# Loading the first block of an output projection unevenly over the DMA engines: 240 of its rows by sixes on 40 partitions

## The chip, the cores and the metric

One core of a Trainium2 chip runs the kernel. The metric is device time in microseconds (us) of one execution. Each comparison alternates the kernel before with the changed one on the same chip. Kernels are compared only within the same rounds. Traces are different: there is one trace of the kernel before.

## The reference, cut to what matters

The program is one decode step: an attention block over a long cache, and a small gated layer, mixed by a gate.

```python
B, Sq, D = 4, 1, 1024
H, Sk, Dh = 32, 8192, 128             # k_cache, v_cache: [B, H, Sk, Dh], 268 MB each, bf16
# wq: [D, H*Dh], wo: [H*Dh, D] (8 MB), w_gate, w_up: [D, 3584], w_down: [3584, D]

q = heads(x @ wq)
p = softmax(q . k_cache * Dh**-0.5)
o = p . v_cache
a = o.reshape(B, Sq, H * Dh) @ wo
b = x + y                             # y: a small gated layer on the same x  (cut)
return g * a + (1 - g) * b            # g = sigmoid(sum(x * gate_w))
```

Nearly all bytes are the two caches: 576 MB are read once, and each is used once. The last things needed are the last rows of v and then all of `wo`, in eight blocks of 1 MB (512 rows).

## The kernel before: the parts that matter

All large loads go into five slots of a ring in SBUF, and are issued by the sync engine in the order of use. A `wo` block lies on all 128 partitions, four rows (8 KB) on each.

```python
    TB = [const.tile([P, CJ * P], BF, name=f"TB{i}") for i in range(3)]   # three 8 KB-wide scratch tiles
    ...                                                                   # of the transposes of K, taken by turns
    def o_rows(g0, g1):                    # puts attention outputs into the row order of wo's blocks
        n = g1 - g0
        lp = small([P, FR, n, Bn])
        for k in range(WB):
            for r in range(FR):
                nc.tensor.matmul(lp[32 * k:32 * k + 32, r], lhsT=identb[:, r:P:FR],
                                 rhs=OT[:, WB * g0 + k:WB * g1:WB, :], start=True, stop=True, skip_group_check=True)
        nc.vector.tensor_copy(out=LT[:, :, g0:g1, :], in_=lp[:])

    def wo_block(g, r0=0, r1=FR):
        ...
        nc.sync.dma_start(out=w[:, r0:r1].rearrange("p r n -> p (r n)"),
                          in_=wov[:, g, r0:r1].rearrange("p r n -> p (r n)"))
        def use():
            for r in range(r0, r1):
                for n in range(NH):
                    mm_acc(acc[:, n * NB:(n + 1) * NB], LT[:, r, g, :], w[:, r, n * NB:(n + 1) * NB])
        return use
    ...
    for kind, d in order:                  # all pairs of K and V
        ...
        if (kind, d) == ("v", ND - 1):
            for g in range(2):
                wo_block(g)()              # blocks 0 and 1: loaded and used ahead of the last V pair
        if kind == "v":
            v_pair(d)
        ...
        if (kind, d) == ("v", ND - 2):
            o_rows(0, GE)
    last = [wo_block(g) for g in range(2, NWB - 2)]
    cuts = [(NWB - 2, 0, 2), (NWB - 2, 2, 4), (NWB - 1, 0, 2), (NWB - 1, 2, 3), (NWB - 1, 3, 4)]
    last += [wo_block(*cut) for cut in cuts]      # the last two blocks in pieces: 512, 512, 512, 256, 256 KB
    ...
    o_rows(GE, NWB)
    for use in last:
        use()
    res = turned(Bn, D)
    nc.vector.tensor_copy(out=res[:, 0:NB], in_=acc[:, 0:NB])
    nc.sync.dma_start(out=out2[:, 0:NB], in_=res[:, 0:NB])
    nc.scalar.copy(out=res[:, NB:D], in_=acc[:, NB:D])
    nc.scalar.dma_start(out=out2[:, NB:D], in_=res[:, NB:D])
```

## Time and profile before

| | before |
|---|---|
| time, median of the first 3 runs | 1343.82 us (1343.58 to 1344.03) |
| span of the profiled run (time 1343.99) | 1342.18 us |
| DMA, mean rate over the span | 429 GB/s |
| PE busy, DVE busy | 77%, 46% of the span |
| last landing of `wo` | 1338.71 us |
| last matmul ends | 1339.37 us |

These are lines of the page of the kernel before. The rows with 40 figures cut the span into equal slices; PEclk is the clock granted to TensorE in tenths. A queue line gives packets, megabytes and the share of the 16 engines' time.

```profile
PEclk9787988888998888889988889888889899888899
DMA  9999999999999999999999999999999999999997
GB/s 414 436 432 431 439 434 427 445 430 422 445 424 430 442 432 426 438 434 428 438 436 426 432 430 434 436 433 438 428 423 436 430 431 442 436 419 444 419 425 325
...
q1 hardware_dynamic: 14276, 575.69, 99.5%
q8 instruction: 27, 0.44, 0.1%
q14 instruction: 5, 0.04, 0.0%
```

The DMA engines are busy in every slice but the last, and one queue (q1, the loads) takes 99.5% of their time. PE and DVE have room on average. So compute does not set the pace of the body, and the change works on the tail. The last two lines are the fetching of instructions, 27 packets of 16 KB and 5 of 8 KB.

This is the chain of waits of the kernel before from 1330 us on: start, duration, what.

```profile
1321.33 16.11 DMA ring<-in_A_wo_dram
1337.43 0.04 issue
1337.47 1.90 PE acc L273 x8
1339.37 0.02 issue
1339.40 0.57 ACT TB L581
```

The last 512 KB and two 256 KB pieces of `wo` decide the end. At 1337.43 the 512 KB piece is complete, eight matmuls follow back to back, then a copy and the store. The last piece lands at 1338.71, and the last two of the eight matmuls start 0.05 us later: that landing is just in time, so both landings bind.

This is the timeline of PE of the kernel before from 1306 us on: start, duration, instruction and count; in brackets the idle time ahead of it and what ended it.

```profile
1306.60 2.75 PE L273 MATMUL acc<-ring,LT 128*4 128x512 bf16 x12 [0.32 <-DVE LT L370]
1308.98 0.39 PE L513 MATMUL o_ps<-ring,PB 128*32 128x512 bf16 x1
...
1313.84 7.07 PE L513 MATMUL o_ps<-ring,PB 128*32 128x512 bf16 x32 [1.23 <-DMA ring<-in_A_v_cache_dram]
1321.31 1.89 PE L513 MATMUL o_ps<-ring,PB 128*32 128x512 bf16 x8 [0.40 <-DMA ring<-in_A_v_cache_dram]
1323.80 1.89 PE L513 MATMUL o_ps<-ring,PB 128*32 128x512 bf16 x8 [0.61 <-DMA ring<-in_A_v_cache_dram]
1326.28 1.89 PE L273 MATMUL acc<-ring,LT 128*4 128x512 bf16 x8 [0.59 <-DMA ring<-in_A_wo_dram]
...
1333.75 5.61 PE L273 MATMUL acc<-ring,LT 128*4 128x512 bf16 x24 [0.36 <-DMA ring<-in_A_wo_dram]
```

PE starts the last V pair at 1308.98 and from there waits for data before nearly every piece: 1.23, 0.40, 0.61, 0.59 and 0.36 us. That idle time is what added PE work may use up.

One thing the page doesn't show is in the trace's landing records. Each DMA engine adds 1 to the transfer's semaphore when its share has landed, and each step has a time. For the last `wo` piece of the kernel before the 16 steps are:

| engines | landed at, us |
|---|---|
| seven, "early" | 1332.27 to 1333.18 |
| one, "middle" | 1335.31 |
| eight, "late" | 1336.93 to 1338.71 |

The piece is usable at the last of these. The spread, 6.4 us, was 0.6 us near the start and grew by about 1.5 us for an engine at each of the 27 fetches of q8; they fell on eight engines, the late ones. The same records point to what made the middle engine: one engine's lag steps from about 0.4 to 1.3, 2.2 and 3.1 us behind the first, in the first transfers to land after three of q14's five fetches (at 108.39, 564.44 and 991.41 us).

### The profile page before, as it was taken

The numbers are of one execution on the slowest core, as the hardware profiler recorded it, in microseconds if no ns is written. First come the engines' busy times: TensorE is split into PE (matmuls) and PEld (weight loads), VectorE is DVE, ScalarE is ACT, GpSimd is POOL, SyncE is SP. The second block draws the span as 40 slices with busy tenths as digits, with TensorE's granted clock in tenths as the row PEclk, the third lists the DMA queues.
The fourth block names the chain that finished last, engine by engine and source line by source line (L and its number), as shares of the span: only waits on it lengthen the run. The fifth ranks groups of instructions, "written<-read, shape, count | busy, mean of one in ns | idle before, by whom it ended". The sixth has DMA issues, their size and how long they took to land.

```text
span 1342.2 us, 7696 instructions
## 1 busy us (share of the span) xinstructions
PE 1032.8 (77%) x4552; PEld 227.9 (17%) x2364; DVE 614.4 (46%) x369; ACT 50.6 (4%) x46; POOL 62.8 (5%) x161
## 2 busy tenths in 40 slices
PE   2565878787788687778977779597778679877898
PEld 0111111111111121111211112111111112111221
DVE  2555655545336554335455556046555254556000
ACT  0000100001000010001000010000100010000100
POOL 2000100001000010001000010000100010000100
PEclk9787988888998888889988889888889899888899
DMA  9999999999999999999999999999999999999997
GB/s 414 436 432 431 439 434 427 445 430 422 445 424 430 442 432 426 438 434 428 438 436 426 432 430 434 436 433 438 428 423 436 430 431 442 436 419 444 419 425 325
DMA packets 14316, 576.18 MB, mean 429 GB/s; under 512 B 1598, under 2 KB 1606, under 8 KB 2252
## 3 DMA queue, kind: packets, MB, share of 16 engines
q1 hardware_dynamic: 14276, 575.69, 99.5%
q8 instruction: 27, 0.44, 0.1%
q14 instruction: 5, 0.04, 0.0%
q10 hardware_dynamic: 8, 0.00, 0.0%
HBM read 575.68 MB, written 0.01 MB: 429 GB/s over the span
## 4 chain that ended last, share of the span: by engine, by line
DMA 66%; DVE 21%; PE 11%; another core or an unknown queue 1%; ACT 0%; issue 0%; SPq 0%; DVEq 0%
DMA ring<-in_A_k_cache_dram 58%; DVE TB L436 21%; PE o_ps L513 9%; DMA ring<-in_A_v_cache_dram 5%; DMA x<-in_gate_w_dram 2%; DMA ring<-in_A_wo_dram 1%; PE S_ps L442 1%; ACT PB L484 0%; PE S_ps L307 0%; PE acc L307 0%; PE acc L273 0%; PE small L533 0%; ACT OS L525 0%; PE small L472 0%
## 5 line engine op out<-in xcount | busy, mean ns | idle before, releaser
L436 DVE STREAM_TRANSPOSE TB<-ring 128x2048 uint32<-128x2048 uint32 x256 | 566.9, 2277 | 492.4 <-DMA ring<-in_A_k_cache_dram 491.5
L442 PE MATMUL S_ps<-TB,Z 128*128 128x512 bf16 x2048 | 518.8, 408 | 219.4 <-DVE TB L436 218.9
L513 PE MATMUL o_ps<-ring,PB 128*32 128x512 bf16 x2048 | 461.4, 388 | 52.6 <-DMA ring<-in_A_v_cache_dram 48.1
L442 PEld LDWEIGHTS <-Z 128*128 128x128 bf16 x1024 | 105.4, 103 | 628.0 <-issue 626.4
L513 PEld LDWEIGHTS <-PB 128*32 128x32 bf16 x1024 | 100.7, 98 | 405.1 <-issue 393.7
L421 POOL COPY Z<-qa 32x4 bf16<-32x4 bf16 x128 | 25.6, 200 | 761.6 <-PE S_ps L442 736.0
L486 POOL COPY PB<-PT 32x1024 bf16<-32x1024 bf16 x16 | 30.3, 1892 | 430.3 <-PE o_ps L513 426.2
L467 ACT ACTIVATE PTs<-S_ps,mx 128x1024 bf16<-128x1024 f32 x8 | 8.9, 1114 | 1020.9 <-DVE mx L463 1020.9
L526 DVE SCALAR_TENSOR_TENSOR OS<-o_ps,mE,OS 128x512 f32<-128x512 f32 x8 | 6.0, 751 | 72.2 <-ACT OS L525 72.2
L484 ACT COPY PB<-PT 32x1024 bf16<-32x1024 bf16 x16 | 30.5, 1908 | 1.5 <-DVE PT L469 1.3
L474 DVE RECIPROCAL rinv<-small 128x16 f32<-128x16 f32 x8 | 2.1, 258 | 42.0 <-PE small L472 42.0
L370 DVE CAST LT<-small 128x64 bf16<-128x64 f32 x2 | 0.4, 224 | 42.3 <-PE small L368 42.3
L236 PE MATMUL small<-identb,x 6*128 6x6 bf16 x8 | 0.6, 195 | 22.3 <-DMA x<-in_gate_w_dram 22.3
L457 DVE TENSOR_REDUCE mx<-S_ps 128x1 f32<-128x1024 f32 x8 | 9.8, 1225 | 15.9 <-PE S_ps L442 15.9
L273 PE MATMUL acc<-ring,LT 128*4 128x512 bf16 x64 | 14.8, 379 | 1.7 <-DMA ring<-in_A_wo_dram 1.0
L469 DVE STREAM_TRANSPOSE PT<-PTs 128x1024 bf16<-128x1024 bf16 x8 | 10.0, 1245 | 10.2 <-ACT PTs L467 10.2
L273 PE MATMUL acc<-ring,hT 128*4 128x512 bf16 x56 | 12.2, 379 | 0.0
L525 ACT ACTIVATE OS<-o_ps,mE 128x512 f32<-128x512 f32 x8 | 5.5, 687 | 162.8 <-PE o_ps L513 162.8
L307 PE MATMUL o_ps<-ring,xw 128*4 128x512 bf16 x56 | 5.7, 536 | 5.3 <-DMA ring<-in_B_w_gate_dram 5.3
L533 PEld LDWEIGHTS small<-selg,OS 128*128 128x128 f32 x64 | 9.0, 208 | 4.1 <-issue 3.9
L533 PE MATMUL small<-selg,OS 128*128 128x16 f32 x64 | 8.7, 269 | 0.0
L238 DVE COPY xw<-small 128x48 bf16<-128x48 bf16 x1 | 0.2, 181 | 15.9 <-PE small L236 15.9
(64 smaller groups left out, 67.2 us busy)
## 6 DMA issues: line engine op xcount, KB each, us to landing
ring<-in_A_k_cache_dram SPq DMA_DIRECT2D x14, 4096.0 KB, 34.1
ring<-in_A_v_cache_dram SPq DMA_DIRECT2D x14, 4096.0 KB, 31.4
ring<-in_B_w_gate_dram SPq DMA_DIRECT2D x1, 7168.0 KB, 37.1
ring<-in_B_w_up_dram SPq DMA_DIRECT2D x1, 7168.0 KB, 39.2
ring<-in_B_w_down_dram SPq DMA_DIRECT2D x2, 3584.0 KB, 27.4
ring<-in_A_wo_dram SPq DMA_DIRECT2D x6, 1024.0 KB, 24.7
ring<-in_A_v_cache_dram SPq DMA_DIRECT2D x2, 2048.0 KB, 28.7
ring<-in_A_v_cache_dram SPq DMA_DIRECT2D x4, 1024.0 KB, 24.7
```

The source lines that it names most:

```text
L273: nc.tensor.matmul(out_ap, lhsT=lhsT, rhs=rhs, start=start, stop=True, skip_group_check=True)
L421: nc.gpsimd.tensor_copy(out=Z[at, :, QP - 1 + QP * q], in_=qa[at, :, h0 + q, b])
L436: nc.vector.transpose(out=flat_t.bitcast(U32), in_=kn[:, c * CJ * Dh:(c + 1) * CJ * Dh].bitcast(U32))
L442: nc.tensor.matmul(sps[:, z, :], lhsT=Z[:, he, s:s + P], rhs=T[:, 16 * z:16 * z + 16, half, :, e], start=(t == 0 and n == 0 and he == 0), ...
L457: nc.vector.tensor_reduce(out=mx[:, 0:1], in_=sps[:].rearrange("p z n -> p (z n)"), axis=AX.X, op=ALU.max)
L467: nc.scalar.activation(out=PTs[:], in_=sps[:].rearrange("p z n -> p (z n)"), func=ACT.Exp, bias=negm[:, 0:1], scale=scale, accum_out=rs[:, ...
L469: nc.vector.transpose(out=PT[:].rearrange("p j i -> p (j i)"), in_=PTs[:])
L484: nc.scalar.copy(out=Bv[at, :, :, q, :], in_=Pv[at])
L486: nc.gpsimd.tensor_copy(out=Bv[at, :, :, q, :], in_=Pv[at])
L513: nc.tensor.matmul(o_ps[row:row + NM, e, :], lhsT=PB[:, RD * t + c, z, w].rearrange("p e s j -> p (e s j)"), rhs=vn[:, j0 * Dh:(j0 + 4) * ...
L526: nc.vector.scalar_tensor_tensor(out=o_sb[:], in0=o_ps[:, 1, :], scalar=mE[:, 1:2], in1=o_sb[:], op0=ALU.mult, op1=ALU.add)
L533: nc.tensor.matmul(oT[:, :], lhsT=o_sb[:, q * Dh:(q + 1) * Dh], rhs=selg[:, q].rearrange("p t s -> p (t s)"), start=(q == 0), stop=(q == 3))
```

## The change

The intent follows from that table. If the early engines carried more of the bytes and the late ones fewer, all could end together. The change cuts `wo`'s first block (512 rows) in three. 240 rows, six to a partition, go on 40 partitions by two transfers whose source is counted in fives, so that only five engines carry them. 16 rows go on 16 partitions, and 256 rows by two on all 128. The wide rows need room, so the three scratch tiles become one. The rows of the attention output must be put in the new order too, by small matmuls with 0/1 matrices (`six`).

```diff
-    TB = [const.tile([P, CJ * P], BF, name=f"TB{i}") for i in range(3)]
+    TB = const.tile([P, 3, CJ * P], BF, name="TB")
@@ opening: 0/1 matrices, made on POOL (cut to its core)
+    six = const.tile([P, 2, 2, SX, 5, 4], BF)
+    ...
+    LX = const.tile([P, SX, Bn], BF)
+    LC = const.tile([16, Bn], BF)
+    L2 = const.tile([P, 2, Bn], BF)
@@ o_rows
+        if g0 == 0:
+            lp = small([P, SX + 3, Bn])
+            for h in range(2):
+                for r in range(SX):
+                    for k in range(2):
+                        nc.tensor.matmul(lp[32 * h:32 * h + 20, r], lhsT=six[:, k, h, r].rearrange("p e o -> p (e o)"),
+                                         rhs=OT[:, k, :], start=(k == 0), stop=(k == 1), skip_group_check=True)
+            ...                            # one matmul for the 16 rows, four for the 256, four copies to LX, LC, L2
+    def wo_first():
+        wo_home[0] = ring[:, slots(1)].rearrange("p (g r n) -> p g r n", g=4, r=FR)
+        n6, half = 40 * SX, P * FR // 2
+        w6 = TB[:].rearrange("p i n -> p (i n)")[:, 0:SX * D]
+        src = A_wo[0:n6].rearrange("(e h o r) n -> h e o (r n)", e=5, h=2, r=SX)
+        for h in range(2):
+            nc.sync.dma_start(out=w6[32 * h:32 * h + 20], in_=src[h])
+        w = wo_home[0][:, 0].rearrange("p r n -> p (r n)")
+        w2, wc = w[:, 0:2 * D], w[0:half - n6, 2 * D:3 * D]
+        nc.sync.dma_start(out=w2, in_=A_wo[half:2 * half].rearrange("(p r) n -> p (r n)", r=2))
+        nc.sync.dma_start(out=wc, in_=A_wo[n6:half])
+        def use():
+            ...                            # 12 matmuls with LX, 4 with L2, 2 with LC, where there were 8
@@ the loop
-            for g in range(2):
-                wo_block(g)()
+            wo_first()()
+            wo_block(1)()
```

The small table `row` of the opening also moves into the shared scratch tile (cut).

More of the change, by code (lines that the diff above doesn't have):

```diff
@@ L169 @@
     turn = [0]
-    TB = [const.tile([P, CJ * P], BF, name=f"TB{i}") for i in range(3)]
+    TB = const.tile([P, 3, CJ * P], BF, name="TB")
     tb_turn = [0]
     def turned(rows, n, dtype=BF):
-        t = TB[tb_turn[0] % 3]
+        t = TB[:, tb_turn[0] % 3]
         tb_turn[0] += 1
@@ L217 @@
     acc = acc4[0:Bn].rearrange("p z n -> p (z n)")
-    row = const.tile([P, 2, 32], F32)
+    row = turned(P, 64, F32).rearrange("p (i n) -> p i n", i=2)
     nc.vector.memset(row[:, 0, 0:1], 0.0)
@@ L233 @@
     nc.vector.tensor_copy(out=identb[:], in_=ident[:])
+    wide = turned(P, 3 * P)
+    nc.gpsimd.memset(wide, 0.0)
+    nc.gpsimd.tensor_copy(out=wide[:, P:2 * P], in_=ident[:])
+    SX = 6
+    six = const.tile([P, 2, 2, SX, 5, 4], BF)
+    for k in range(2):
+        for h in range(2):
+            at = P * (1 - k)
+            nc.gpsimd.tensor_copy(out=six[:, k, h], in_=wide[:, at:at + 240].rearrange("p (e h o r) -> p h r e o", e=5, h=2, o=4)[:, h])
+    LX = const.tile([P, SX, Bn], BF)
+    nc.gpsimd.memset(LX[:], 0.0)
+    LC = const.tile([16, Bn], BF)
+    L2 = const.tile([P, 2, Bn], BF)
     xw_ps = small([P, DT, NX], BF)
@@ L370, in o_rows @@
         nc.vector.tensor_copy(out=LT[:, :, g0:g1, :], in_=lp[:])
-    wo_home = {}
+        if g0 == 0:
+            lp = small([P, SX + 3, Bn])
+            for h in range(2):
+                for r in range(SX):
+                    for k in range(2):
+                        nc.tensor.matmul(lp[32 * h:32 * h + 20, r], lhsT=six[:, k, h, r].rearrange("p e o -> p (e o)"),
+                                         rhs=OT[:, k, :], start=(k == 0), stop=(k == 1), skip_group_check=True)
+            nc.tensor.matmul(lp[0:16, SX], lhsT=identb[:, P - 16:P], rhs=OT[:, 1, :], start=True, stop=True, skip_group_check=True)
+            for k in range(2):
+                for r in range(2):
+                    nc.tensor.matmul(lp[64 * k:64 * k + 64, SX + 1 + r], lhsT=identb[:, r:P:2], rhs=OT[:, 2 + k, :],
+                                     start=True, stop=True, skip_group_check=True)
+            for h in range(2):
+                nc.vector.tensor_copy(out=LX[32 * h:32 * h + 20], in_=lp[32 * h:32 * h + 20, 0:SX])
+            nc.vector.tensor_copy(out=LC[:], in_=lp[0:16, SX])
+            nc.vector.tensor_copy(out=L2[:], in_=lp[:, SX + 1:SX + 3])
@@ new lines @@
+    wo_home = {}
+    def wo_first():
[3 more added lines that the diff above has]
+        src = A_wo[0:n6].rearrange("(e h o r) n -> h e o (r n)", e=5, h=2, r=SX)
+        for h in range(2):
+            nc.sync.dma_start(out=w6[32 * h:32 * h + 20], in_=src[h])
[4 more added lines that the diff above has]
+        def use():
+            for r in range(SX):
+                for n in range(NH):
+                    mm_acc(acc[:, n * NB:(n + 1) * NB], LX[0:52, r, :], w6[0:52, r * D + n * NB:r * D + (n + 1) * NB])
+            for r in range(2):
+                for n in range(NH):
+                    mm_acc(acc[:, n * NB:(n + 1) * NB], L2[:, r, :], w2[:, r * D + n * NB:r * D + (n + 1) * NB])
+            for n in range(NH):
+                mm_acc(acc[:, n * NB:(n + 1) * NB], LC[:], wc[:, n * NB:(n + 1) * NB])
+        return use
```

## The prediction

> **What bounds the kernel now.** DMA: the page's slices show the 16 DMA engines 90% or more busy in all but the last, queue q1 at 99.5%, 429 GB/s; PE is busy 77%, DVE 46%. Only the tail can give time back. There the chain of waits is DMA wo to 1337.43 us, eight acc matmuls to 1339.37, a cast of 0.57, the store.
>
> The engines do not finish together. The trace's landing records (16 semaphore steps a transfer) show the last wo piece landing on seven engines at 1332.27 to 1333.18, on one at 1335.31, on eight at 1336.93 to 1338.71. That spread of 6.4 us was 0.6 at 38 us and grew in steps of about 1.5, one at each of the 27 instruction fetches (queue q8, 16 KB each): a data packet starts about 1.05 us late and takes 0.5 longer. They rotate over eight engines, the late eight. (The Trainium skill, "Runtime: NRT & Kernel Launch", Instruction fetch mechanics: blocks of 256 instructions, 16 KiB; the 27 packets agree.)
>
> **What the change does.** It loads the early engines more and the late ones less. The Trainium skill, "DMA: Bandwidth & Descriptors", Why a DMA increments its semaphore by 16: a sync-queue transfer runs on the largest number up to 16 that divides the slowest dimension of both sides, on the lowest-numbered engines. 20 partitions and fives give engines 0 to 4. The opening loads of x (4 and 1 landings) mark low engines: following their packets, I place three of engines 0 to 3 among those without fetches; the fourth is ambiguous.
>
> Wo's first MB per engine, by packet times (8 KB 0.31 us, 16 KB 0.61, 4 KB 0.16, 2 KB 0.08):
> - before: eight of 8 KB, 2.5 us.
> - after: engines 0 to 4 take eight of 12 KB (estimate 0.46 each), eight of 4 KB, one of 2 KB: 5.0; the others 1.36.
>
> The late eight end 1.1 us earlier (1337.6), engines 0 to 4 2.5 later (1334.8 to 1335.7), still before them. DMA gain: 1.1 us, all on the critical path.
>
> **What it adds.** PE: 29 small matmuls with weight loads (16 now take 0.65 us: estimate 1.2), four DVE copies of 0.2 (0.3 exposed), 18 accumulating matmuls instead of 8 at 0.2155: 2.2. PE starts the last V pair about 3.7 us later than 1309. Its slack there: idle 1.23, 0.40, 0.61, 0.59, then about 0.6 for each MB of wo. By that the lag is nearly gone at the last piece: the last matmul ends at 1338.3 (DMA) to 1338.8 (PE), against 1339.37. The main loop is unchanged: transposes wait on PE as with three separate buffers. The opening PoolE work hides under the first load. Eight semaphores reused over three more transfers still leave a backlog.
>
> **Predicted: 1343.0 us, range 1342.3 to 1344.0.** Chances: faster by over 2% 0.003, within 2% 0.992, slower 0.005.
>
> **What would show it.** Last piece's landings: two engines at 1331.8, one near 1334, five at 1335, eight to 1337.6, in place of 7/1/8. The w6 transfers: five landings each, 12 KB packets near 0.46 us. Still 27 fetches, the last some 8 us earlier. PE: waits in the last V pair (1.23, 0.40, 0.61) gone, those on the last wo pieces small. Main loop unchanged.
>
> **What would make it wrong.** If engines 0 to 4 hold a late one, the end moves out 2.5 us (about 1346). If PE's lag does not drain (throttled clock; it was full from 1268 on), the gain is lost: about 1344. If PE's lag is smaller, 1342.7.

## The result, and the profile after

| | before | after |
|---|---|---|
| time, median of 6 runs | 1343.86 us | 1343.82 us |
| range | 1343.58 to 1344.03 | 1343.67 to 1345.18 |
| span of the profiled run | 1342.18 | 1341.69 |
| its time | 1343.99 | 1343.71 |

The ratio is 1.0002, with a 95% interval of 0.9989 to 1.0015: the same. The time lies inside the predicted range, which says little, since the range holds the old time too. The forecast was a gain of 0.8 us, and hardly any came.

The page of the changed kernel, the same lines:

```profile
PEclk9787989988998898899988889898889799889999
DMA  9999999999999999999999999999999999999998
GB/s 415 438 430 431 439 434 426 438 430 428 436 432 429 439 434 424 440 430 436 436 426 432 432 432 438 436 427 431 436 424 435 436 427 445 431 423 434 429 422 334
...
q1 hardware_dynamic: 14358, 575.69, 99.5%
q8 instruction: 27, 0.44, 0.1%
```

The body is unchanged, the bytes are the same, there are still 27 fetches on q8. The DMA issues from 1270 us on show the new transfers (count, KB each; before there were three of 512 KB, and none of the last two lines):

```profile
ring<-in_A_wo_dram SPq DMA_DIRECT2D x4, 512.0 KB, 23.6
...
TB<-in_A_wo_dram SPq DMA_DIRECT2D x2, 240.0 KB
ring<-in_A_wo_dram SPq DMA_DIRECT2D x1, 32.0 KB, 28.3
```

The chain of waits of the changed kernel from 1330 us on:

```profile
1320.64 16.08 DMA ring<-in_A_wo_dram
1336.71 0.04 issue
1336.76 1.90 PE acc L287 x8
1338.66 0.02 issue
1338.68 0.57 ACT TB L636
```

It is the same chain, 0.72 us earlier at the DMA (1337.43 to 1336.71) and 0.71 at the end of PE. So the DMA did gain something. The timeline of PE:

```profile
1306.63 0.23 PE L395 MATMUL small<-OT,identb 128*64 128x4 bf16 x4
1307.32 2.75 PE L287 MATMUL acc<-TB,LX 52*4 52x512 bf16 x12 [0.46 <-DVE LX L398]
...
1312.12 0.39 PE L568 MATMUL o_ps<-ring,PB 128*32 128x512 bf16 x1
...
1313.00 12.90 PE L568 MATMUL o_ps<-ring,PB 128*32 128x512 bf16 x59
...
1331.08 7.57 PE L287 MATMUL acc<-ring,LT 128*4 128x512 bf16 x32 [0.36 <-DVE LT L384]
```

PE starts the last V pair at 1312.12, 3.1 us later than before (predicted: about 3.7), and the waits for V data are gone: 59 matmuls run through where there were 1.23, 0.40 and 0.61 us of idle. In the last group, 32 matmuls spaced 0.2155 us with a last one of 0.38 would take 7.06 us if they waited for nothing, and they take 7.57. So PE has about 0.5 us of waiting left, and the DMA still sets the end.

The landing records of the last `wo` piece:

| engines | before, us | after, us |
|---|---|---|
| early | seven at 1332.27 to 1333.18 | three, not used by the new rows, at 1331.37 to 1331.70 |
| the "middle" one | 1335.31 | **1338.00**, the last of all |
| late, the three last of them | to 1338.71 | 1337.39, 1337.59, 1337.68 |
| the other nine (late ones and early ones now loaded) | | 1335.33 to 1336.32 |

The late engines end 1.03 us earlier, as predicted (1337.6 forecast, 1337.68 measured). But the middle engine moved out by 2.69 us and is now last. So the landing gain is 0.71 us in this trace in place of 1.1.

The profiled pair also shows where that 0.71 us went. The span gained only 0.48 us, and the time only 0.28 us:

| step | before | after | change |
|---|---|---|---|
| last matmul ends | 1339.37 | 1338.66 | -0.71 |
| store landed to the sync engine's closing drain | 0.08 | 0.32 | +0.24 |
| time minus span | 1.80 | 2.02 | +0.22 |

(Time minus span is the mean over the runs of both kernels; in the profiled pair alone it is 1.82 and 2.02.) At the end the sync engine waits for the eight DMA semaphores in turn, by number, 101 to 105 and 108 to 110. Before, the two output stores were on 109 and 110, the last of the list. The three extra transfers turned the assignment on by three, the stores are on 102 and 103, and the remaining waits come after the store has landed.

So the theory (A) is: the placement of the middle engine cost the DMA part of its gain, and 0.24 us inside the span and 0.22 us outside it (time minus span; whether before or behind it, no trace shows) ate the rest. The rival is (B): PE, which got about 3 us more work, is what keeps the end. (C) is no rival but the part of A about the end: that the closing waits come from the semaphores' order alone.

### The profile page after: what moved, and what is told of

The parts are those of the page before. It is cut to its first block, busy times and chain, and to the rows that moved or that the text cites. A ratio compares the mean times of both kernels' runs of the same rounds, so it can differ in the third digit from the quotient of the medians.

```text
span 1341.7 us, 7789 instructions
## 1 busy us (share of the span) xinstructions
PE 1038.0 (77%) x4591; PEld 228.6 (17%) x2398; DVE 615.2 (46%) x373; ACT 50.6 (4%) x46; POOL 64.6 (5%) x168
## 4 chain that ended last, share of the span: by engine, by line
DMA 68%; DVE 20%; PE 11%; ACT 0%; issue 0%; SPq 0%; DVEq 0%
DMA ring<-in_A_k_cache_dram 58%; DVE TB L491 20%; PE o_ps L568 8%; DMA ring<-in_A_v_cache_dram 6%; DMA ring<-in_B_w_gate_dram 3%; PE S_ps L497 2%; DMA ring<-in_A_wo_dram 1%; PE o_ps L321 0%; ACT PB L539 0%; PE acc L321 0%; PE acc L287 0%; PE small L588 0%; ACT OS L580 0%; PE small L527 0%; SPq L560 0%
## 5 line engine op out<-in xcount | busy, mean ns | idle before, releaser
L491 DVE STREAM_TRANSPOSE TB<-ring 128x2048 uint32<-128x2048 uint32 x256 | 566.8, 2277 | 490.8 <-DMA ring<-in_A_k_cache_dram 490.8
```

The source lines that it names most:

```text
L491: nc.vector.transpose(out=flat_t.bitcast(U32), in_=kn[:, c * CJ * Dh:(c + 1) * CJ * Dh].bitcast(U32))
```

## The experiments

Eighteen kernels ran, in five lots. Each lot shares its runs of the kernel before.

### First lot: repeat, engine ruler, PE alone, DMA alone

**a1_after_again**: the changed kernel once more.

> The changed kernel once more, for a second trace and an interval. Theory A (one of engines 0 to 4 is the middle engine of before, and with 2.7 us more it becomes the last one): the last wo piece lands last on that engine, near 1338.0, the late eight by 1337.7, and the time is 0.5 to 0.7 us under before. Theory B (the matmul work that was added takes the gain): the last landing is as early, but the last matmul ends more than 0.66 us after it. If the medians differ by under 0.2 us while the trace's end is 0.5 earlier, something outside the traced span or a spread between runs takes the rest.

Measured: median 1343.96 us against 1343.88 before (ratio 0.9999, 0.9986 to 1.0013; all five runs, 1343.68 to 1344.11). The middle engine is again last, at 1338.35, and the late ones end at 1337.97. In the chain the DMA ends at 1337.07. So the gain of the DMA in this run is only 0.36 us, and the end costs 0.25 and 0.21 again: the three sum to +0.1, as measured. The 0.5 to 0.7 us under before that I expected of the time did not come. The DMA gain of one and the same kernel thus varies by about 0.35 us from trace to trace.

**a2_ruler**: which engine is the middle one? The kernel before, with eight small loads of 1 to 8 partitions, ahead of `wo`. A load of k partitions is carried by the k lowest-numbered engines (the Trainium skill, "DMA: Bandwidth & Descriptors", Why a DMA increments its semaphore by 16; here the loads of 1 to 8 partitions indeed show that many landings; the numbers of the engines are the page's, the trace has only the landings).

```diff
+            for i, k in enumerate((1, 2, 3, 4, 5, 6, 7, 8)):
+                nc.sync.dma_start(out=TB[i // 4][0:k, (i % 4) * D:(i % 4 + 1) * D], in_=A_wo[0:k])
```

> The kernel before with eight tiny loads in front of wo, 1 to 8 partitions of 2 KB, so that each lands on 1 to 8 engines, counted from the lowest if the rule holds. Each landing time places one engine among the sixteen of the transfer before. Theory A: among engines 0 to 4 four stand with the early seven and one with the middle engine, about 3.0 us behind; no engine of 0 to 7 but that is late. Rival (all five early): engines 0 to 4 all within 0.9 us of the first. Time within 1 us of before.

Measured: one run, 1347.94 us, 4.1 us over before, where I had expected 1 at most. The loads of 1, 2 and 3 partitions have all landed by 1294.27; the load of 4 has three landings with those and a fourth at 1295.61. So engine 3 is the middle engine. The load of 5 adds an early landing at 1293.54: engine 4 is early. The loads of 6 and 7 add landings at 1299.18 and 1297.36: engines 5 and 6 are late. My expectation on the last point was a miss. In one respect this run cannot serve: the sync engine waited for the ruler loads, the engines fell into step, and the spread of the `wo` transfers that followed collapsed from 6.5 to 0.65 us (1.6 to 1.8 in the last six, after one more fetch). The time rose all the same.

**a3_pe_only**: all the added PE, DVE and POOL work, with the DMA of before. Five rows of zero weights (`L0`) stand in for the extra matmuls, so the result stays right.

```diff
-            for g in range(2):
-                wo_block(g)()
+            wo_first()()      # the old single transfer of block 0, its 8 matmuls, and 10 more with L0 = 0
+            wo_block(1)()
```

> Wo's first block loaded as before in one transfer, but with all matmuls, copies and setup of the change (10 of the 18 accumulating matmuls have zero weights, so the result is right). Theory A: the added matmul work drains in the tail, last matmul about 0.66 us after the last landing, time within 0.2 us of before. Theory B: 0.5 to 0.8 us slower than before.

Measured: median 1343.88, the same as before (ratio 1.0000, 0.9988 to 1.0013); the last landing is at 1338.63, the DMA in the chain ends at 1337.35, time minus span is 1.81. The PE work costs nothing at the DMA's old pace. This speaks against B.

**a4_dma_only**: the DMA of the changed kernel, with the matmuls of before. The result is wrong: block 0's matmuls read rows in the wrong places.

```diff
-        if g0 == 0:
-            ...                                 # all small matmuls and copies for LX, LC, L2
-            for r in range(SX):
-                ...                             # LX, L2 and LC matmuls
+            wr = wo_home[0][:, 0]
+            for r in range(FR):
+                for n in range(NH):
+                    mm_acc(acc[:, n * NB:(n + 1) * NB], LT[:, r, 0, :], wr[:, r, n * NB:(n + 1) * NB])
```

> The four transfers of the change, but no added matmuls: the block is used as before from the ring, which holds other data there, so the result is wrong on purpose. Theory A: no better than the changed kernel, 0.5 to 0.7 us under before in the trace, last landing at 1338.0 on the middle engine. Theory B: 0.5 us or more faster than the changed kernel of the same rounds.

Measured: median 1343.94 (ratio 1.0000, 0.9987 to 1.0012), no better than the changed kernel. The last landing is at 1338.27 on the middle engine, the chain's DMA ends at 1336.99, time minus span is 2.03. So without any of the added PE work the gain is missing just as well. B is refuted for this change: the loss lies in the DMA and in the end.

### Second lot: the end, the middle engine, PE's lag

**b1_after_plus5** and **b2_before_plus3**: tiny loads that nothing reads, long before the end, shift only which semaphores the stores get. Five in the changed kernel put them back on 109 and 110; three in the kernel before put them on 102 and 103.

```diff
+    idle = const.tile([1, 5, 16], BF)
+    def tiny():
+        for i in range(5):                      # range(3) in the kernel before
+            nc.sync.dma_start(out=idle[:, i], in_=A_wo[i:i + 1, 0:16])
@@ the loop
+        if (kind, d) == ("k", 12):
+            tiny()
```

> The changed kernel with five loads of 32 bytes in mid-run, so that it issues eight transfers more than before in place of three, and its two stores signal on the last two of the eight transfer semaphores again, as before. Theory C (the end costs more when the stores' semaphores stand earlier in the order in which the end waits for them): the sync engine's last waits after the stores land shrink by 0.25 us, time minus traced span returns from 2.02 to 1.80 us, and the time is 0.4 to 0.5 us under the changed kernel: 1343.4 to 1343.5. Rival (the gain is lost elsewhere): unchanged, 1343.8 to 1344.0.

> The kernel before with three loads of 32 bytes in mid-run: nothing else of the change. Theory C: the stores' semaphores move as in the change; last waits 0.25 us longer, time minus span 2.02 us, time 0.4 to 0.5 us over before: 1344.3 to 1344.4. Rival: same as before, 1343.9.

Measured: b1 has a median of 1343.51 against 1343.91 for the kernel before of these rounds (ratio 0.9997, 0.9984 to 1.0009). From the landed store to the drain it is 0.08 us again. b2 has a mean of 1344.22 against 1343.94, +0.28, with its waits at the end back (0.32 us), and time minus span at 1.78. So the in-span part of C is shown both ways: 0.25 us from nothing but a shifted order. The later runs happen to give the steps between: from the landed store to the drain it is 0.08 us with the stores' semaphores not shifted, 0.19 with a shift by one (c1, d2, d3), 0.25 by two (d1), 0.32 by three and 0.34 by four (d6). The other part fell: time minus span of b1 is 2.016, not back to 1.80. That 0.22 us is not the store's semaphore.

The chain of b1 from 1330 us on, to compare with the changed kernel (1336.71):

```profile
1320.68 16.07 DMA ring<-in_A_wo_dram
1336.75 0.04 issue
1336.79 1.90 PE acc L287 x8
```

**b3_threes**: does it help to spare engine 3? The same with fewer engines: 192 rows by eights on 24 partitions, source in threes (engines 0 to 2), 64 rows on 64 partitions, the five tiny loads, and the small matmuls one V pair earlier.

```diff
-    SX = 6
-    six = const.tile([P, 2, 2, SX, 5, 4], BF)
+    SX = 8
+    six = const.tile([P, 2, 2, SX, 3, 4], BF)
-        n6, half = 40 * SX, P * FR // 2
+        n6, half = 24 * SX, P * FR // 2
-            nc.sync.dma_start(out=w6[32 * h:32 * h + 20], in_=src[h])
+            nc.sync.dma_start(out=w6[32 * h:32 * h + 12], in_=src[h])
@@ and 64 rows for LC, with the five tiny loads
-        if (kind, d) == ("v", ND - 2):
+        if (kind, d) == ("v", ND - 3):
             o_rows(0, GE)
```

> Twelve partitions a transfer with a source in threes, so three engines (0 to 2) and not the middle engine 3: 192 rows by eights on 24 partitions, 64 rows on 64 partitions; its small matmuls moved one V pair earlier, where PE waits anyway; five tiny loads for the semaphores. Theory A: w6 lands three times, all within 0.9 us; the middle engine stays about 3.2 us behind the first; the last landing is on a late engine with four fetches, 0.9 us earlier than before, near 1337.8; engines 0 to 2 near 1337.2. With theory C time 1342.9 to 1343.2. If PE's lag now matters, the last matmul ends more than 0.7 us after the last landing.

Measured: 1344.23 median (ratio 1.0004), a miss. What A says of the engines held: three landings within 0.96 us, the middle engine untouched at +3.02. But the last landing is at 1338.56 on a late engine (1337.8 expected): the late ones did not come forward. The rate shows a loss. These are windows of one microsecond; the last two figures of each line are the DMA engines' busy share and GB/s. The kernel before:

```profile
1298.00:1299.00 1.00, 0.00 (x0) 0.00 (x0) 0.00 (x0) 0.00 (x0) 0.00 (x0) 1.00 0.99 418
1299.00:1300.00 1.00, 0.93 (x5) 0.19 (x2) 0.00 (x0) 0.00 (x0) 0.00 (x0) 1.00 0.94 393
1300.00:1301.00 1.00, 1.00 (x6) 0.19 (x2) 0.00 (x0) 0.00 (x0) 0.00 (x0) 1.00 1.09 459
```

And b3_threes:

```profile
1298.00:1299.00 1.00, 1.00 (x7) 0.19 (x2) 0.00 (x0) 0.00 (x0) 0.00 (x0) 1.00 1.22 348
1299.00:1300.00 1.00, 1.00 (x6) 0.19 (x2) 0.00 (x0) 0.00 (x0) 0.00 (x0) 1.00 0.84 262
1300.00:1301.00 1.00, 1.00 (x6) 0.29 (x3) 0.00 (x0) 0.00 (x0) 0.00 (x0) 1.00 0.97 320
```

The engines stay busy but move 930 KB in place of 1270 in these 3 us. The packets of 8 KB in these 3 us took a median of 0.406 us, 0.313 in the kernel before. At 429 GB/s the missing 340 KB are, as an estimate, 0.8 us of the whole core's DMA, about what the redistribution was to win. The changed kernel moved 1231 KB there. Of what differs from it, two things are suspected: the 64 rows on 64 partitions, and the step of 128 KB from one engine's source rows to the next one's (96 KB in the change). c2 and c3 below pick that up.

**b4_early**: b1, with the small matmuls one V pair earlier. If PE's lag were the loss, taking about a microsecond from it would show.

```diff
-        if (kind, d) == ("v", ND - 2):
+        if (kind, d) == ("v", ND - 3):
             o_rows(0, GE)
```

> As b1, with the small matmuls and copies of the change one V pair earlier, where PE waits for data. PE's lag at the last V pair shrinks by about 1.5 us. If that lag costs nothing (theory A) same as b1 within 0.15 us; if PE's lag costs (theory B) 0.2 us or more under b1.

Measured: median 1343.46 (ratio 0.9996, 0.9984 to 1.0009), within 0.1 us of b1. PE's lag is not the loss. In this trace the middle engine's offset was smaller, 2.68 us when the new transfers began, and the last landing, 1337.79, is the earliest of the five traces with exactly these transfers (1337.79 to 1338.35). In these five the last landing follows the middle engine's offset in the V transfer just ahead of the new ones:

| | b4 | b1 | change | a4 | a1 |
|---|---|---|---|---|---|
| middle engine behind the first, us | 2.68 | 3.05 | 3.11 | 3.29 | 3.43 |
| last landing of `wo`, us | 1337.79 | 1338.02 | 1338.00 | 1338.27 | 1338.35 |

That is what A asks for, and the 0.35 us between traces go with it. Why the offset varies is open.

b1 and b4 are the best versions found. Each of their ten runs (at most 1343.62) is below each of the nine runs of the kernel before of the same rounds (at least 1343.69). The means differ by 0.44 and 0.48 us, 0.03 to 0.04%, which is inside the formal interval of the ratio.

### Third lot: which engines, which shape

**c1_shape_probe**: one tiny load of 20 partitions with its source in fives, in the kernel before. Does that shape alone lengthen the time outside the span?

```diff
+    idle3 = const.tile([20, 8], BF)
+    def tiny():
+        src = A_wo[0:240].rearrange("(e h o r) n -> h e o (r n)", e=5, h=2, r=6)
+        nc.sync.dma_start(out=idle3[:], in_=src[0][:, :, 0:8])
```

> The kernel before with one tiny load in mid-run, of the shape of the change's w6 transfers (20 partitions, source in fives, 16 bytes a partition). It asks whether that shape alone makes the end after the traced span longer. If it does: time minus span 2.02 us. If not: 1.80 us, and the longer end belongs to something else in the changed transfers. The stores' semaphores move by one, so the span itself may grow by 0.1 to 0.25 us.

Measured: median 1343.96 us, the same as before; time minus span 1.80. The shape alone does not.

**c2_fours**: engines 0 to 3: 192 rows by sixes on 32 partitions, and 64 rows on 64 partitions as in b3. The tiny loads and the early small matmuls are kept in all of c2, c3 and c4.

```diff
-    six = const.tile([P, 2, 2, SX, 5, 4], BF)
+    six = const.tile([P, 2, 2, SX, 4, 4], BF)
-        n6, half = 40 * SX, P * FR // 2
+        n6, half = 32 * SX, P * FR // 2
-            nc.sync.dma_start(out=w6[32 * h:32 * h + 20], in_=src[h])
+            nc.sync.dma_start(out=w6[32 * h:32 * h + 16], in_=src[h])
```

> Sixteen partitions a transfer, source in fours: engines 0 to 3, 192 rows by sixes on 32 partitions, 64 rows on 64 partitions; small matmuls early, five tiny loads. Theory A: w6 lands four times, the fourth about 2.5 to 3 us behind, so the middle engine is one of 0 to 3, and it is last, near 1338.0. For the miss of the threes: if loading 64 rows to 64 partitions was what slowed all engines there (port theory), the slump of the bandwidth between 1298 and 1301 us comes again, and the late engines end 0.5 us or more after 1337.8; if it was the source's step of 128 KB (step theory; here 96), the bandwidth stays above 360 GB/s and they end by 1337.9.

Measured: median 1344.73 against 1343.96 (ratio 1.0005). The first two transfers have four landings, the fourth 3.55 and 3.81 us behind the first: the middle engine is one of 0 to 3, which agrees with the ruler. It is last again, at 1339.34. The rate sags again at the same place:

```profile
1298.00:1299.00 1.00, 0.71 (x4) 0.10 (x2) 0.00 (x0) 0.00 (x0) 0.00 (x0) 1.00 1.08 354
1299.00:1300.00 1.00, 0.41 (x2) 0.10 (x1) 0.00 (x0) 0.00 (x0) 0.00 (x0) 1.00 0.90 322
1300.00:1301.00 1.00, 1.00 (x6) 0.19 (x2) 0.00 (x0) 0.00 (x0) 0.00 (x0) 1.00 1.11 406
```

**c3_threes10**: engines 0 to 2 again, but the 240 rows of the change, by tens on 24 partitions, and only 16 rows on 16 partitions.

```diff
-    SX = 6
-    six = const.tile([P, 2, 2, SX, 5, 4], BF)
+    SX = 10
+    six = const.tile([P, 2, 2, SX, 3, 4], BF)
-        n6, half = 40 * SX, P * FR // 2
+        n6, half = 24 * SX, P * FR // 2
```

> Threes again, but 240 rows by tens on 24 partitions and the other 16 rows on 16 partitions as in the change. Theory A: the middle engine keeps 3.0 us; engines 0 to 2 take 5.0 us more and land between 1337.3 and 1338.2. Port theory: no slump below 360 GB/s from 1298 to 1301, the late engines end by 1337.7, time 1343.2 to 1343.6. Step theory: also none (step 160 KB). If the slump comes, few engines reading large rows are the cause.

Measured: median 1344.01 of six runs, 1343.77 to 1349.85, against 1343.96. Expected was 1343.2 to 1343.6: a miss. The deep sag is gone (342, 440 and 410 GB/s in the three windows, 1192 KB together, where b3 had 930 and c2 1082), and the middle engine stays at +3.30. The source's step is 128 KB in b3, 96 in c2 and 160 in c3, so it does not sort them. The sag goes with the 64 rows on 64 partitions, a transfer that is also four times as large as the 16 rows of c3. The Trainium skill, "SBUF — State Buffer", Door 1, says that the partitions a transfer spans decide how many of the 16 ports into the memory it reaches, and that partitions 0 to 63 reach half of them. The sag with b3 and c2 fits this. But the 16 partitions of c3 reach fewer ports still and carry a quarter of the bytes, so ports and size are not told apart; that the ports are the cause was not tested by itself.

The profiled run of c3 happens to be the one of 1349.85, so its trace tells little about the end, but it shows another danger. Windows of it (the figure before the DMA share is the granted clock):

```profile
1260.00:1300.00 40.00, 38.92 (x219) 10.94 (x145) 1.08 (x6) 0.98 (x1) 0.41 (x1) 0.85 1.00 424
1300.00:1313.00 13.00, 13.00 (x62) 2.75 (x30) 0.00 (x0) 0.00 (x0) 0.00 (x0) 1.00 1.00 423
1313.00:1320.00 7.00, 7.00 (x23) 1.05 (x11) 0.00 (x0) 0.00 (x0) 0.00 (x0) 0.52 1.01 418
```

The clock was halved for 7 us in the very stretch in which PE must catch up, and it was low from 1260 to 1300 too (0.85; 0.96 in b4). The last landing was at 1338.15, but PE ended at 1345.03, 6.9 us behind it. This is one run. That the other single slow runs (1345.18 of the changed kernel, 1345.03 of b3, 1345.33 of c3) have the same reason is not known, since they were not profiled. Their mean clocks of 0.897 to 0.901 are ordinary, but 7 us at half the clock change such a mean by less than 0.003.

**c4_mixed**: a split load: 120 rows by sixes in fives, 120 rows by tens in threes, so that engine 3 gets half as many extra bytes.

```diff
-    six = const.tile([P, 2, 2, SX, 5, 4], BF)
+    SH = ((5, 6), (3, 10))
+    six = const.tile([P, 2, 2, 120], BF)
...
+        for h, (e, r) in enumerate(SH):
+            src = A_wo[120 * h:120 * h + 120].rearrange("(o e r) n -> e o (r n)", o=4, e=e)
+            nc.sync.dma_start(out=w6[32 * h:32 * h + 4 * e, 0:r * D], in_=src)
```

> The first 120 rows by sixes in fives (engines 0 to 4), the next 120 by tens in threes (engines 0 to 2), so the middle engine 3 gets only one of the two; other rows as in the change; small matmuls early, five tiny loads. Theory A: middle engine ends near 1336.2, engines 0 to 2 by 1337.2, last landing on a late engine near 1337.65, 1.05 us before that of before; with the end 0.22 us longer the time is 1343.0 to 1343.2, under b4. Rival: 1343.4 or more.

Measured: median 1343.87 (1343.44 to 1344.36) against 1343.96, expected 1343.0 to 1343.2: a miss. On the DMA it did what it should: the last landing is at 1337.79 on a late engine, 0.92 us earlier than before, and the middle engine is no longer last. But the chain now holds no DMA at its end:

```profile
1331.55 7.08 PE acc L290 x32
1338.63 0.02 issue
```

32 matmuls run back to back for 7.08 us, which is the time that 32 need without any wait. The 26 matmuls that the mixed first block takes (18 in the change) have pushed PE behind: PE starts the last V pair at 1312.60, in b4, with 18, at 1311.01. It ends 0.84 us after the last landing. So here rival B is true. Its size in this trace is 0.18 us: b4 has its last landing at 1337.79 as well and ends at 1338.45. But the profiled run is the fastest of the five, so what keeps the median 0.4 us above it is not shown. The room for added PE work ends between the change and c4. c3 has the same 26 matmuls, so its miss may have this cause too; none of its ordinary runs was profiled.

### Fourth and fifth lot: what lengthens the time outside the span

Time minus span is 2.01 to 2.05 us in the changed kernel, a1, a4, b1, b3, b4, c2, c3 and c4, and 1.78 to 1.81 in the kernel before, a2, a3, b2 and c1. So it goes with the changed transfers. The last six runs added these to the kernel before one kind at a time (two rows-by-six transfers, halves, 16 rows), then together; extra rows are read by nothing.

```diff
+            dead = TB6[:, 0:6 * D]                                     # d1, d4, d5, d6
+            src = A_wo[0:240].rearrange("(e h o r) n -> h e o (r n)", e=5, h=2, r=6)
+            for h in range(2):
+                nc.sync.dma_start(out=dead[32 * h:32 * h + 20], in_=src[h])
+            nc.sync.dma_start(out=TB6[0:16, 0:D], in_=A_wo[240:256])   # d3; in d4 and d6 into a free part of TB
+            for i in range(2):                                         # d2, d5, d6: block 0 in two halves
+                nc.sync.dma_start(out=w[:, 2 * i * D:2 * (i + 1) * D],
+                                  in_=wov[:, 0, 2 * i:2 * (i + 1)].rearrange("p r n -> p (r n)"))
```

> The kernel before with the two transfers of 240 rows by sixes added, into a tile that nothing reads. Time minus span: 2.02 us if these two carry the longer end, 1.80 if not; I lean to 2.02, because they are the only ones with packets of 12 KB. The time itself rises by about 1 us on the early engines only and is not the point: 1343.5 to 1347.5. Engines 0 to 4 should again land fives, with one about 3 us behind the others.

> The kernel before with wo's first block brought by two transfers of 512 KB instead of one of 1 MB. Time minus span: 1.80 us if halves are innocent, 2.02 if they carry the longer end; I lean to 1.80. Time within 0.5 us of the kernel before.

> The kernel before with one transfer of 16 rows on 16 partitions (2 KB each) added, into a tile that nothing reads. Time minus span: 1.80 us if it is innocent, 2.02 if it carries the longer end; I lean to 1.80. Time within 0.5 us of the kernel before.

> The kernel before with the two transfers by sixes and the 16-row transfer added, read by nothing. Time minus span: 2.02 us if the number of large added transfers carries the longer end, 1.80 if the halves are needed. I lean to 1.80. Time 1343.9 to 1345.

> The kernel before with the two transfers by sixes added, and wo's first block in two halves. Three transfers more, as in the change. Time minus span: 2.02 us if three large transfers more are what it takes, 1.80 if the 16-row one is needed too. I lean to 2.02. Time 1343.9 to 1345.

> The kernel before with the sixes and the 16 rows added and the first block in halves: every kind of transfer of the change, and all of the old bytes. Time minus span: 2.02 us if the transfers together carry the longer end; 1.80 would mean that it is not their kinds but the order of landings that they leave, or something that I have not listed. I lean to 2.02. Time 1343.9 to 1345.

| kernel | time, one run | time minus span of its trace |
|---|---|---|
| d1_w6_extra | 1344.42 | 1.78 |
| d2_two_halves | 1343.95 | 1.81 |
| d3_wc_extra | 1344.29 | 1.78 |
| d4_w6_wc | 1344.90 | 1.80 |
| d5_w6_halves | 1344.35 | 1.81 |
| d6_all_extra | 1345.04 | 1.78 |

None shows 2.02, not even all kinds together. I had leaned to 2.02 for d1, d5 and d6; all three are misses. What the changed kernels have and d6 hasn't is that block 0's old rows are not loaded by the old shapes as well: the 256 rows lie by two on each partition, from consecutive rows, and less is loaded altogether. They also have the new set-up of the opening (`six` and the tiles beside it), which only a3 had without the transfers; the two together are not tested on the kernel before. I have no mechanism that would follow from any of this. The 0.22 us outside the span stays open: it is measured in nine runs, it is not the store's semaphore (b1, b2), not the PE work (a3, a4), not a small load of that shape (c1) and not one of the transfers by kind (d1 to d6).

d1 does show one thing more: its two transfers again land five times each, the last of the five 2.9 us behind the first.

## Why the prediction was wrong

- **What bounds the kernel: right.** The DMA, and in the tail the late engines. The chain is the same after.
- **The late eight end 1.1 us earlier, at 1337.6: right.** 1337.68 in the changed kernel, 1.03 us earlier; 1337.97, 0.74 earlier, in the repeat.
- **"Engines 0 to 4 2.5 later (1334.8 to 1335.7), still before them": this step failed.** The extra time was sized right (2.69 us measured on the middle engine; the 12 KB packets took a median of 0.4655 us, 0.46 estimated). The placement was not. Engine 3 is the middle one, which stood 3.04 us behind the first before the change. 1335.31 + 2.69 = 1338.00, and that is the last landing. The prediction called the fourth engine ambiguous, but feared only a late one (about 1346), and left out the engine that it had itself listed at 1335.31. The gain was 0.71 us in the profiled run, 0.36 and 0.44 in a1 and a4 (0.68 and 0.92 in b1 and b4), in place of 1.1. The ruler (a2) and the four landings of c2 place it on engine 3.
- **"All on the critical path": the second step that failed.** A landing 0.71 us earlier did end the last matmul 0.71 us earlier. But the closing waits took 0.24 back, because three more transfers moved the stores to the front of the order in which the semaphores are waited for: shown by b1 and b2. 0.22 more went outside the span, its cause open. In the profiled run this step cost 0.44 us, the first one 0.39 (1.1 less 0.71). The sum for the profiled pair, -0.71 + 0.24 + 0.20, gives the -0.28 us measured, up to rounding. For the repeat a1, -0.36 + 0.25 + 0.21 gives +0.10, and its median lies 0.08 above.
- **PE: right.** The lag at the last V pair was 3.1 us (about 3.7 predicted), the waits of 1.23, 0.40 and 0.61 us are gone, and the last matmul ended at 1338.66, inside the 1338.3 to 1338.8 predicted. That hit is partly luck: the range ran from a DMA limit of 1338.3 to a PE limit of 1338.8, and it was the DMA, 0.36 later than predicted, that fell into it. a3 and b4 show that the lag is not the loss here. c4 shows that eight accumulating matmuls more make it one, of 0.18 us.
- **Main loop unchanged: right.** The last V pair but one lands at 1299.07 in both to within 0.05 us, and the transposes take 566.8 us in all against 566.9.
- **Fetches: 27, the last some 8 us earlier.** 27 it was on q8; the last came at 1317.74 in place of 1330.68, 13 us earlier. The size was off and nothing hung on it.

## What to carry to other kernels

Before loading some DMA engines more than others, find every engine's place by its landings, with small loads of 1, 2, 3 and more partitions if need be; an engine in the middle can become the last. A gain below a microsecond at the end is easily lost to things that have nothing to do with the data: here to the order of the closing waits, which a few tiny dead loads put right for 0.25 us. And a change that adds work to a second engine in the tail uses up room that a slower clock in one run, or a few matmuls more, will need.

## What the Trainium skill lacked or had wrong

- "DMA: Bandwidth & Descriptors", Why a DMA increments its semaphore by 16: the rule for the number of engines holds here (5, 4 and 3 landings for sources in fives, fours and threes). That they are the lowest-numbered ones no trace here can show, since it has no engine numbers.
- "DMA: Bandwidth & Descriptors", Latency and other measured facts: it names only engines 7 and 15 as usually slower in traces, with a guess that concerns transfers issued by GpSimd. Here the large loads are issued by the sync engine, and eight engines are late by 4.7 to 6.4 us, with 5 and 6 among them by the ruler. The lag grows by about 1.5 us at each 16 KB instruction fetch on an engine, and by 0.9 us at each 8 KB one on the middle engine. The page does not have this.
- "Runtime: NRT & Kernel Launch", Instruction fetch mechanics: the blocks of 16 KB agree (27 packets), but it calls the cost "mostly hidden". For the DMA engines it isn't: three or four fetches on each of the eight late engines make up most of the 6.4 us of spread. What that costs in time, no run here isolates.
- No page that I read says that the waits at a kernel's end depend on which semaphores the last transfers got (0.08 to 0.34 us from landed store to drain), nor what makes the time outside the traced span 1.80 or 2.02 us.
- "SBUF — State Buffer", Door 1: it gives the bandwidth of a transfer on 64 partitions by itself, and does not say that such a transfer slows others beside it. In b3, with 64 rows on 64 partitions, the 8 KB packets of the next block took 0.406 us in place of 0.313, and three windows moved 930 KB (1082 in c2, 1231 in the change).
